# Attention and a gated feed-forward on one core: the product with T of six chunks in seven half products

## The chip, the core and the metric

The kernel runs on one core of a Trainium2 chip. The metric is the device time of one execution in microseconds. Before the change three runs gave a median of 410.5 us (409.81 to 410.56).

An instruction runs on one of five engines, each with its own queue that is served in order: TensorE (PE in the profile; its weight loads are PEld), VectorE (DVE), ScalarE (ACT), GpSimd (POOL) and SyncE (SP). SP, POOL and ACT also issue DMAs from their queues. TensorE writes to PSUM, which is read here by VectorE and ScalarE. GpSimd works on SBUF only.

## What is computed

Eight batches of eight heads, 1152 keys, and queries that are averaged in pairs (576 per batch and head), head size 64. The attention's result, 4608 tokens by 512, goes through a gated feed-forward:

```python
q_pool = q.reshape(B, H, S // 2, 2, D).mean(axis=3)
scores = scale * q_pool @ k.T
attn   = exp(scores - max) / sum
x      = attn @ v                 # as 4608 x 512
out    = (((x @ w1) * (x @ w2)) @ w3) @ w_out
```

w1 and w2 are 512 x 1024, w3 is 1024 x 1024, w_out 1024 x 512. The kernel multiplies T = w3 @ w_out once (1024 x 512), so that each token needs g = (x w1)(x w2), elementwise, and then g T.

## The kernel before, in words

**Attention.** Heads are taken in 32 pairs. The scores of all pairs form one long row of 32 x 9 x 576 columns, cut into 324 slots of 512. `scores` (L434) computes one slot for both heads of a pair into one of three double banks of PSUM (tag psc), and ScalarE writes the exponentials to a ring in SBUF (L448). An AV group (`av_mm`, L461) multiplies the ring with v: 18 matmuls of 65 columns (L474), or 36 for the rest tiles (L471). There are 144. VectorE normalizes each (L495 to L509), and a transpose turns the result into xT, on TensorE for the first pairs (L516, L519, copies L527 and L529), by a DMA on SP's queue from pair 8 on (`x_dma`, L485).

**Loads.** `prepare(p)` (L878) is written out at the start of pair p - 2. On GpSimd it casts K (L355), adds the query pairs (L359, L361) and casts V (L368). It issues the loads of V for pair p and of K and Q for p + 2, from GpSimd's queue for the first pairs, from SP's later. SP also turns K and Q by DMA (`transp`, L375).

**Feed-forward.** The 4608 tokens are nine chunks of 512 (CH). For chunks 0 to 6 (LATE is 7) `moe_groups(c)` (L597) yields steps: for each of eight blocks ft of 128 hidden columns, x w1 and x w2 (L583, 4 matmuls of 512 columns each), the first copied by VectorE (L610), the second multiplied with it into the gate tile g (L614); then four products g T for 128 tokens each (L621, 8 matmuls of 512 columns, called a step of size 2), scaled by VectorE (L630) and stored by GpSimd's queue (L595; for chunk 5 SP's, for chunk 6 SP's in pieces). T itself comes from `t_groups` (L544) ahead of chunk 0. Chunks 7 and 8 are done at the end by `late_chunks` (L683) in a form with seven half products for four (Strassen-Winograd): it needs sums of the four quarters of w1 and w2 (`weight_sums`, L649), of T (the tS tiles) and of x (`x_sums`, L670), all on GpSimd. The weight and T sums stand in one block at the start of pair 30.

**Order.** `_visits` (L184) is a planner that runs when the kernel is built. A visit is three score slots and then a string of A (an AV group), P (a pair's transposes on TensorE), m or s (a feed-forward step into the single bank mo, or into a bank of the scores). A beam search chooses the strings by the costs in `_Plan` (L115): time of TensorE, and when banks come free from VectorE and ScalarE. GpSimd and the DMA queues are not in it. The list `fills` (L920) gives each step's size; `free` says how many steps may be drawn after so many AV groups: a chunk's steps count as released when the tokens of the chunk are normalized and, with DMA transposes, four groups later. The steps themselves come from the generators in `queue`; `fill` (L831) takes the next, gives it a bank, issues its matmuls and then its VectorE work. What is left when the visits end is drawn between the last AV groups, and the rest behind them.

Tiles with a tag share buffers: a new one waits until all readers of the one `bufs` earlier are done (g8 holds the gates, two of them; kst, vst, qst the loads, two each).

Of the kernel before, what the change touches and what calls it, by code (L numbers as in the profile page):

```python
# [183 lines left out]
def _visits(n, start, units, pairs, fills, free, ready, width):  # L184
# [8 lines left out]
    for vis in range(n):  # L193
# [12 lines left out]
        def step(p, seq, na, f, pr, t0):  # L206
            d = p.t - t0
            loose = free[na] if vis >= start else 0
            if pr == len(ats) and (na >= len(units) or units[na][3] > vis) and (d > 1.0 or f >= loose):
                end(p, seq, na, f)  # L210
            if d > 2.3 or len(seq) > 4:
                return
            if pr < len(ats):
                q = p.copy()
                q.pair(ats[pr])
                step(q, seq + "P", na, f, pr + 1, t0)
            if na < len(units) and units[na][2] <= vis and seq.count("A") < 3:
                q = p.copy()
                q.av_group(*units[na][:2])
                step(q, seq + "A", na + 1, f, pr, t0)  # L220
            if f < loose:
                for b in "ms":
                    q = p.copy()
                    q.fill(fills[f][0], fills[f][1], b == "s")
                    step(q, seq + b, na, f + 1, pr, t0)
# [40 lines left out]
def kernel(  # L266
# [277 lines left out]
    def t_groups():  # L544
        w3T = {}

        def turn(ft):
            def go(pt):
                w3T[ft] = msb.tile([128, NF, 128], FP16, tag="w3T", bufs=2, name="w3T")
# [22 lines left out]
    CH = 512  # L572

# [22 lines left out]

    def moe_groups(c):  # L597
        t = {}

# [12 lines left out]
        for ft in range(NF):  # L612
            def gate(pb, ft=ft):
                nc.vector.tensor_tensor(out=t["g"][:, ft, :], in0=pb, in1=t["a"], op=ALU.mult)  # L614

            yield 1, lambda pa, ft=ft: first(pa, ft), keep, 0.0
            yield 1, lambda pb, ft=ft: proj(pb, w2sb, ft, c), gate, 0.0
# [23 lines left out]
    HF, HM, HC = NF // 2, dm // 2, CH // 2  # L641
    LATE = B * Sq // CH - 2
    IS = 1.0 / (SCL * SCL)
    wS, tS, xS = [], {}, {}
# [4 lines left out]
    def weight_sums():  # L649
        for w, tag in ((w1sb, "kst"), (w2sb, "vst")):  # L650
# [4 lines left out]
            nc.gpsimd.tensor_tensor(out=s1, in0=a21, in1=a22, op=ALU.add)  # L655
            minus(s2, s1, a11)
            minus(s3, a11, a21)
            minus(s4, a12, s2)
            wS.append({1: a11, 2: a12, 3: s4, 4: a22, 5: s1, 6: s2, 7: s3})
        b11, b12 = T16[:, 0:HF, 0:HM], T16[:, 0:HF, HM:dm]  # L660
        b21, b22 = T16[:, HF:NF, 0:HM], T16[:, HF:NF, HM:dm]
        st = [att.tile([128, 2, HF, HM], FP16, tag="qst", name="tS") for _ in range(2)]
        t1, t2, t3, t4 = st[0][:, 0], st[0][:, 1], st[1][:, 0], st[1][:, 1]
        minus(t1, b12, b11)
        minus(t2, b22, t1)
        minus(t3, b22, b12)
        minus(t4, b21, t2)
        tS.update({1: b11, 2: b21, 3: b22, 4: t4, 5: t1, 6: t2, 7: t3})

    def x_sums():  # L670
        st = msb.tile([128, 2, 4, NC // 2, HC], FP16, tag="wo", bufs=1, name="xS")
        for c in (0, 1):
            (_, a, n), = runs(LATE + c)
            b11, b12 = xT[:, 0:NC // 2, a:a + HC], xT[:, 0:NC // 2, a + HC:a + n]
            b21, b22 = xT[:, NC // 2:NC, a:a + HC], xT[:, NC // 2:NC, a + HC:a + n]
            x1, x2, x3, x4 = (st[:, c, i] for i in range(4))
# [154 lines left out]
    def fill(scored=False):  # L831
        if not head():
            return False
        n, go, put, at = ahead.pop(0)
        pt = bank(scored) if put else None
        go(pt)
        if put:
            put(pt)
        return True
# [19 lines left out]
    for _ in range(33):  # L859
# [61 lines left out]
    for ft in range(0, NF, 2):  # L921
        fills += [(0.5, W3_AT[ft // 2])] * 2 + [(1, WO_AT)] * 4
    free = []
    for n in range(NU + 1):
        for c in loose.get(n, []):
            fills += [(1, 0.0)] * (2 * NF) + [(2, 0.0)] * (CH // 128)
# [13 lines left out]
    def av_step():  # L940
# [9 lines left out]
        if p >= XD and t == QM - 1:  # L950
            x_dma(p)
        release()
# [102 lines left out]
```

## Time and profile before

| | us |
|---|---|
| median of 3 runs | 410.5 (409.81 to 410.56) |
| the profiled execution | 411.45 |
| its span, first to last instruction | 409.8 |
| TensorE busy | 396.8 (97%) |
| ScalarE busy | 335.2 (82%) |
| VectorE busy | 218.7 (53%) |
| GpSimd busy | 212.8 (52%) |
| matmuls of the product with T, L621 (192 in the main part, 32 in the last) | 45.6 and 7.2 |
| mean granted clock of TensorE | 0.998 |

Span and shares are of the profiled execution, which took 0.95 us more than the median of the runs; a difference worked out from the trace is taken from the median. Busy time of matmuls overlaps, since one begins before the one ahead has ended; so the distance from start to start is what a matmul takes of the engine's time. The profile's first part gives busy time by engine, its fourth the chain of work that ended last, its fifth groups of instructions by line: times executed, busy time, mean length of one, and the idle time of the engine just ahead of them with what ended it. The timeline lists merged instructions in order of time; the windows give busy time by stage.

### The profile page before, as it was taken

Reading aid. Unit: us, or ns where it says so; the run is one execution under the profiler, and the core shown is the slowest. Engines: PE = TensorE matmul, PEld = TensorE weight load, DVE = VectorE, ACT = ScalarE, POOL = GpSimd, SP = SyncE. Lnnn points to the kernel's source line nnn. Section 1 sums busy time; section 2 is a strip of 40 time slices with the busy share of each in tenths; the row PEclk is TensorE's granted clock in tenths of the full one; section 3 lists DMA queues with packets and bytes.
Section 4 is the critical chain, followed back from the end, with each engine's and each line's share of the span. In section 5 each row is a group of like instructions: output and inputs, shape, how many; then the busy total and the mean of one; then the engine's idle time right before and its main releaser. Section 6 shows DMA issues by size and latency. Waiting matters only on the chain.

```text
span 409.8 us, 13190 instructions
## 1 busy us (share of the span) xinstructions
PE 396.8 (97%) x5506; PEld 261.6 (64%) x5506; DVE 218.7 (53%) x594; ACT 335.2 (82%) x380; POOL 212.8 (52%) x237
## 2 busy tenths in 40 slices
PE   5899999999999999999999999999999999999995
PEld 3477887565555655565556556655777655658884
DVE  1255565665355534654355536553546435765993
ACT  4978979898889998999989999999899889107752
POOL 5789966470664225504533336333633897051860
PEclk9999999999999999999999999999999999999999
DMA  8999999999598899949999999996998170121005
GB/s 278 251 308 268 274 289 304 346 238 292 173 265 228 198 283 249 260 114 248 245 277 261 250 304 255 259 321 144 278 241 180 26 151 19 22 62 50 9 26 183
DMA packets 94079, 86.35 MB, mean 211 GB/s; under 512 B 60096, under 2 KB 68544, under 8 KB 94016
## 3 DMA queue, kind: packets, MB, share of 16 engines
q1 hardware_dynamic: 84480, 60.11, 61.3%
q0 software_dynamic: 8384, 24.06, 21.1%
q10 hardware_dynamic: 1152, 1.31, 0.9%
q8 instruction: 43, 0.70, 0.7%
q14 instruction: 20, 0.16, 0.1%
HBM read 67.11 MB, written 9.44 MB: 187 GB/s over the span
## 4 chain that ended last, share of the span: by engine, by line
PE 88%; DMA 6%; POOL 2%; ACT 1%; issue 1%; DVE 1%; SPq 0%; ACTq 0%
PE psc L443 19%; PE avb L474 16%; PE mo L583 15%; PE mo L621 10%; PE mot L583 9%; PE b L724 7%; PE mo L561 3%; DMA qst<-in_q_dram 3%; PE avb L471 3%; DMA xT<-xb 3%; PE b L621 2%; PE mo L724 1%; PE ptk L383 1%; ACT ring L448 1%; DMA kst<-in_k_dram 1%; PE avb L724 1%
## 5 line engine op out<-in xcount | busy, mean ns | idle before, releaser
L448 ACT ACTIVATE ring<-psc 128x1024 f16<-128x1024 f32 x324 | 308.2, 1025 | 34.5 <-PE psc L443 32.7
L474 PEld LDWEIGHTS <-ring 128*128 128x128 f16 x2304 | 84.4, 98 | 26.3 <-issue 7.1
L443 PE MATMUL psc<-kqT 64*128 64x512 f16 (+7 forms) x1152 | 96.2, 290 | 3.6 <-ACT ring L448 0.9
L474 PE MATMUL avb<-vaug,ring 128*128 128x65 f16 x2304 | 91.4, 193 | 0.0
L355 POOL CAST kq<-kst 128x1152 f16<-128x1152 f32 x31 | 35.7, 1152 | 77.1 <-DMA kqT<-kq 52.9
L443 PEld LDWEIGHTS <-kqT 64*128 64x128 f16 x1152 | 45.8, 95 | 31.2 <-issue 8.5
L621 PE MATMUL mo<-T,gT 128*128 128x512 f16 x192 | 45.6, 380 | 0.0
L495 DVE RECIPROCAL rzall<-avb 128x2 f32<-128x2 f32 x144 | 23.8, 165 | 37.0 <-PE avb L474 20.3
L630 DVE TENSOR_SCALAR osb<-mo 128x512 f32<-128x512 f32 x24 | 16.6, 692 | 48.6 <-PE mo L621 48.6
L359 POOL TENSOR_TENSOR kq<-qst 128x512 f16<-128x512 f32 x31 | 39.4, 1272 | 1.1 <-DMA qst<-in_q_dram 1.1
L368 POOL CAST vaug<-vst 128x1152 f16<-128x1152 f32 x32 | 36.6, 1143 | 5.8 <-PE psc L443 5.3
L595 POOL DMA_DIRECT2D out_dram<-osb x18 | 9.9, 552 | 55.9 <-DVE rzall L495 55.9
L614 DVE TENSOR_TENSOR gT<-mo,asb 128x512 f16<-128x512 f32 x36 | 24.9, 692 | 24.7 <-PE mo L583 24.4
L583 PE MATMUL mo<-xT,w2sb 128*128 128x512 f16 (+2 forms) x168 | 37.2, 350 | 0.0
L621 PEld LDWEIGHTS <-gT 128*128 128x128 f16 x224 | 19.8, 98 | 25.5 <-issue 5.2
L610 DVE COPY asb<-mo 128x512 f32<-128x512 f32 x32 | 22.1, 691 | 25.2 <-PE mo L583 24.9
L583 PEld LDWEIGHTS <-w2sb 128*128 128x128 f16 x256 | 21.9, 97 | 20.8 <-issue 4.2
L583 PEld LDWEIGHTS <-w1sb 128*128 128x128 f16 x256 | 22.0, 97 | 20.4 <-issue 3.9
L583 PE MATMUL mo<-xT,w1sb 128*128 128x512 f16 (+2 forms) x148 | 33.3, 351 | 1.1 <-DMA xT<-xb 1.1
L509 DVE TENSOR_TENSOR xb<-avb,rzall 128x128 f16<-128x128 f32 x96 | 28.0, 291 | 3.3
L583 PE MATMUL mot<-xT,w1sb 128*128 128x512 f16 (+1 forms) x104 | 23.6, 354 | 0.1
L583 PE MATMUL mot<-xT,w2sb 128*128 128x512 f16 (+1 forms) x84 | 19.5, 359 | 0.0
(143 smaller groups left out, 432.7 us busy)
## 6 DMA issues: line engine op xcount, KB each, us to landing
vst<-in_v_dram SPq DMA_DIRECT2D x25, 576.0 KB, 5.0
kst<-in_k_dram SPq DMA_DIRECT2D x23, 576.0 KB, 5.8
qst<-in_q_dram SPq DMA_DIRECT2D x23, 512.0 KB, 7.3
kst<-in_k_dram POOLq DMA_DIRECT2D x8, 576.0 KB, 9.9
out_dram<-osb POOLq DMA_DIRECT2D x18, 256.0 KB, 6.1
qst<-in_q_dram POOLq DMA_DIRECT2D x8, 512.0 KB, 10.6
vst<-in_v_dram POOLq DMA_DIRECT2D x7, 576.0 KB, 6.9
w3c<-in_moe_w_dram POOLq DMA_DIRECT2D x4, 512.0 KB, 8.2
```

Source lines behind the costliest of these rows:

```text
L355: nc.gpsimd.tensor_copy(out=kq16[:, 0:NJ].rearrange("p c u d -> p u c d"), in_=kst.rearrange("p u (c d) -> p u c d", d=D))
L359: eng.tensor_tensor(out=kq16[:, NJ:NJ + QM].rearrange("p c u d -> p u c d"), in0=qv[:, :, :, 0], in1=qv[:, :, :, 1], op=ALU.add)
L368: nc.gpsimd.tensor_copy(out=va[:, :, :, 0:D], in_=vs.pop(p).rearrange("p u (c d) -> p u c d", d=D))
L443: nc.tensor.matmul(psc[:, u, f - s * G:f - s * G + ln], kT2[u * 64:u * 64 + 64, jt, :], qpT[u * 64:u * 64 + 64, i0:i0 + ln], start=True, s ...
L448: nc.scalar.activation(out=ring[:, :, r0:r0 + G], in_=psc, func=AF.Exp, bias=0.0, scale=SCALE)
L474: nc.tensor.matmul(avb[:, o + u * E1:o + u * E1 + E1], ring[:, u, c0:c0 + 128], va[:, u, jt, :], start=(jt == 0 and u == 0), stop=(jt == N ...
L495: nc.vector.reciprocal(out=rzall[:, i, :], in_=av[:, :, D:E1].rearrange("p u o -> p (u o)"))
L509: nc.vector.tensor_tensor(out=xbt, in0=av[:, :, 0:D], in1=rzall[:, i, :].unsqueeze(2).to_broadcast([128, 2, D]), op=ALU.mult)
L583: nc.tensor.matmul(pw[:, d0:d0 + n], wt[:, mc, ft * 128:ft * 128 + 128], xT[:, mc, a:a + n], start=(mc == 0 and d0 == 0), stop=(mc == NC - ...
L614: nc.vector.tensor_tensor(out=t["g"][:, ft, :], in0=pb, in1=t["a"], op=ALU.mult)
L621: nc.tensor.matmul(po, t["g"][:, ft, tt:tt + 128], T16[:, ft, :], start=(ft == 0), stop=(ft == NF - 1))
L724: nc.tensor.matmul(pt[:, n * f:n * f + n], l[:, i, :], b[:, i, :], start=(p in (1, 5) and f == 0 and i == 0), stop=(i == kc - 1), skip_gro ...
```

## The change

The product with T of chunks 0 to 5 (`seven`) becomes seven products of 256 tokens by 256 columns over half the hidden columns: two blocks of 128 tokens, four matmuls of 256 columns each, in one bank. Product 1 is drawn behind gate 4, and products 2, 6, 7, 4, 5, 3 behind the first two steps of the next chunk (`LAG`). Sums of the gates are made on GpSimd, in place in g but for s1: behind gate 5 for two blocks, behind gates 6 and 7 for one, and a fourth sum behind product 2. Product 3 adds to the bank of product 5 after that has been read; both go to the bank mo ("m"). VectorE reads each product out with one operation, and each quarter of the chunk's output is stored from GpSimd's queue (`store_two`, one DMA for two blocks of 128 tokens where they lie together). The planner's list has 17 steps of size 1 for chunk 0, 23 for chunks 1 to 5, and 22 of size 1 with 4 of size 2 for chunk 6.

The T sums move to chunk 0's first four gates, the eight weight sums are issued one behind each AV group from pair 30 on. The T sums lie in the tile of w_out, the x sums in those of the Q loads. The matmuls that run ahead of the first transposes are 15 instead of 33.

```diff
@@ _visits
-                for b in "ms":
+                for b in fills[f][2]:
@@ moe_groups
+        lagged, late_fills[:] = late_fills[:], []
+        seven = c < LATE - 1
...
+        def product(pt, a, n, start=True):
+            for u in range(2):
+                for f in range(HF):
+                    nc.tensor.matmul(pt[:, u * HM:u * HM + HM], a[:, f, u * 128:u * 128 + 128], tS[n][:, f, :],
+                                     start=(start and u == 0 and f == 0), stop=(f == HF - 1), skip_group_check=True)
+
+        def plus(out, pt, x):
+            nc.vector.scalar_tensor_tensor(out=out, in0=two(pt), scalar=IS, in1=x, op0=ALU.mult, op1=ALU.add)
...
+        def quarter(h, n, pt, x):
+            osb = msb.tile([128, 2, HM], FP32, tag="osb", bufs=3, name="osb")
+            plus(osb, pt, x)
+            store_two(nc.gpsimd, c * CH + h * HC, osb, slice(n * HM, n * HM + HM))
...
+        def sums(f, n):
...
+            nc.gpsimd.tensor_tensor(out=s1, in0=a21, in1=a22, op=ALU.add)
+            minus(a21, a11, a21)
+            minus(a11, s1, a11)
+
+        def half(fts):
+            for ft in fts:
+                def gate(pb, ft=ft):
+                    nc.vector.tensor_tensor(out=t["g"][:, ft, :], in0=pb, in1=t["a"], op=ALU.mult)
+                    if c == 0 and ft < HF:
+                        t_sum(ft)
+                    if seven and ft > HF:
+                        sums(*((0, 2) if ft == HF + 1 else (ft - HF, 1)))
...
+                if 2 * ft + 2 == LAG:
+                    yield from lagged
+
+        yield from half(range(HF + 1))
+        if seven:
+            yield 1, lambda pt: product(pt, t["g"][:, 0:HF, 0:HC], 1), p1, 0.0
+        yield from half(range(HF + 1, NF))
...
+            def p2(pt):
+                quarter(0, 0, pt, t["p"])
+                for f in range(0, HF, 2):
+                    minus(g[:, HF + f:HF + f + 2, lo], g[:, HF + f:HF + f + 2, lo], g[:, f:f + 2, lo])
...
+            late_fills.extend((
+                (1, lambda pt: product(pt, g[:, HF:NF, lo], 2), p2, 0.0),
+                (1, lambda pt: product(pt, g[:, 0:HF, lo], 6), lambda pt: plus(t["p"], pt, t["p"]), 0.0),
+                (1, lambda pt: product(pt, g[:, 0:HF, hi], 7), p7, 0.0),
+                (1, lambda pt: product(pt, g[:, HF:NF, hi], 4), lambda pt: quarter(1, 0, pt, t["z"]), 0.0),
+                (1, p5, lambda pt: quarter(1, 1, pt, t["z"]), 0.0),
+                (1, lambda pt: product(t["bank"], g[:, HF:NF, lo], 3, False),
+                 lambda pt: quarter(0, 1, t["bank"], t["p"]), None),
+            ))
+            return
@@ weight_sums, one from av_step ahead of release()
+    def weight_sum():
+        if todo:
+            o, x, y, op = todo.pop(0)
+            nc.gpsimd.tensor_tensor(out=o, in0=x, in1=y, op=op)
@@ the matmuls ahead of the first transposes
-    for _ in range(33):
+    for _ in range(15):
@@ fills
-            fills += [(1, 0.0)] * (2 * NF) + [(2, 0.0)] * (CH // 128)
+            step = [(1, 0.0, "ms")]
+            rest = step * 4 + [(1, 0.0, "m")] * 2
+            fills += step * LAG + (rest if c else []) + step * (2 * NF - LAG)
+            fills += step if c < LATE - 1 else [(2, 0.0, "ms")] * (CH // 128)
```

## The prediction on record

> **What bounds the kernel now.** I read the shares first, then the chain that ended last, then the order of work in time on TensorE. In the page's first part:
>
> ```profile
> PE 396.8 (97%) x5506; PEld 261.6 (64%) x5506; DVE 218.7 (53%) x594; ACT 335.2 (82%) x380; POOL 212.8 (52%) x237
> ...
> PE 88%; DMA 6%; POOL 2%; ACT 1%; issue 1%; DVE 1%; SPq 0%; ACTq 0%
> ...
> L448 ACT ACTIVATE ring<-psc 128x1024 f16<-128x1024 f32 x324 | 308.2, 1025 | 34.5 <-PE psc L443 32.7
> ```
>
> PE is busy nearly throughout, the chain (second line) lies on PE for 88%, and ScalarE's exponentials wait 32.7 us for PE, not the other way round. A busy PE need not be a streaming PE, so I look at PE's timeline over one chunk's products with T:
>
> ```profile
> 99.39 1.90 PE L621 MATMUL mo<-T,gT 128*128 128x512 f16 x8
> 101.12 0.71 PE L474 MATMUL avb<-vaug,ring 128*128 128x65 f16 x18
> 101.67 0.22 PE L519 MATMUL avb<-both,xbc 128*128 128x64 f16 x2
> 101.83 0.83 PE L443 MATMUL psc<-kqT 64*128 64x384 f16 x10
> 102.58 1.90 PE L621 MATMUL mo<-T,gT 128*128 128x512 f16 x8
> 104.32 0.71 PE L474 MATMUL avb<-vaug,ring 128*128 128x65 f16 x18
> ```
>
> The columns are start and length; the ends are modelled, so the starts count. A visit (three score slots, one product, one AV group) repeats after 102.58 - 99.39 = 3.19 us and has no gap: 1.74 product, 0.55 AV, about 0.15 turn, 0.76 scores. A visit costs what PE does in it. Then the windows, cut at the starts of the chunks' first projections (66.14, 111.42, ...):
>
> ```profile
> 66.14:111.42 45.28, 45.14 (x620) 26.63 (x618) 25.44 (x76) 40.19 (x43) 23.48 (x27) 1.00 0.94 264
> 111.42:157.95 46.53, 46.42 (x678) 28.21 (x677) 23.56 (x69) 42.67 (x46) 18.22 (x21) 1.00 1.00 235
> 157.95:201.80 43.85, 43.76 (x611) 26.07 (x609) 22.12 (x61) 39.97 (x43) 19.68 (x22) 1.00 0.97 238
> ...
> 246.53:290.01 43.48, 43.48 (x614) 26.08 (x612) 22.05 (x61) 39.98 (x43) 19.44 (x23) 1.00 0.97 243
> ...
> 336.61:368.06 31.45, 31.45 (x379) 17.85 (x376) 20.08 (x55) 11.95 (x14) 14.73 (x11) 1.00 0.13 35
> ```
>
> After the window come its length and PE, PEld, DVE, ACT, POOL. PE has at most 0.14 us idle in each of these rows. From 290.01 to 336.61 it is the same; only at 205 us does PE stand, 1.06 us, for the transposed x of chunk 3. So a microsecond of PE work taken out is worth a microsecond, as long as ScalarE, banks and GpSimd keep up.
>
> **The change, step by step.** *Products.* Four products of 8 matmuls by 512 columns leave each of six chunks; seven of 8 by 256 come. From starts, the old one takes 1.74 us (102.58 to 104.32), four 6.95. The same shape as the new one runs at L561 (8 by 256; 61.59 to 62.47, 0.88) and L724 (four from 396.01 to 396.45, 0.109 each, 0.87 for 8):
>
> ```profile
> 61.59 1.04 PE L561 MATMUL mo<-wosb,w3T 128*128 128x256 f16 x8
> 62.47 0.71 PE L474 MATMUL avb<-vaug,ring 128*128 128x65 f16 x18
> ...
> 396.01 0.60 PE L724 MATMUL b<-tS,gT 128*128 128x256 f16 x4
> 396.45 0.60 PE L724 MATMUL b<-tS,room 128*128 128x256 f16 x4
> ```
>
> Seven are 6.16, so 0.79 goes per chunk, 4.7 us in six. There are 24 more weight loads per chunk; L724 has one for each matmul, and it shows at neither line.
>
> On this the Trainium skill speaks against the change: "TensorE: Matmul & The Clock Gate", Back-to-back issue gap, gives 131 ns for each matmul of 512 columns and 81 for 128 in a stream with weight loads. By it, 32 old matmuls would be 4.2 us and 56 new ones (about 98 ns between the two figures, an estimate) 5.5, a loss of 1.3 per chunk. The trace disagrees: 1.74 / 8 = 217 ns at 512 columns and 109 at 256.
>
> *Where the work goes.* Products 2 to 7 of a chunk are drawn two steps into the next. Counted in steps of 0.87, chunk 0's stretch goes from 24 to 17, those of 1 to 5 from 24 to 23, chunk 6's from 24 to 30. The windows of chunks 1 to 5 begin right behind the AV group that releases the chunk (groups 35, 57, 75, 93 and 111, counted in PE's timeline and held against the release counts in the code), so the planner already spends a chunk's steps by the next release, and shorter stretches are taken in full unless ScalarE is late next. ScalarE does six exponentials in 5.60 us (timeline from 10.87), 0.933 each, 2.80 per visit. Stretches of 13.5 visits need 37.8 and would have 42.6: covered. Chunk 0's has 14 visits, 39.2 on ScalarE, and 45.28 - 7 x 0.87 = 39.2 on PE: level. I take 0.5 us lost there, bounds 0 and 3.5 (below).
>
> *Evictions.* Seven instead of four, 0.69 each (L630, L614), 12.4 us on VectorE in all. A visit of two one-step fills (112.17 to 115.37, 3.20) takes as long as one with a two-step product, so more evictions and banks cost nothing there. Products 5 and 3 share a bank: product 3 waits for 5's eviction (0.2 + 0.69), hidden by an AV group and scores (0.55 + 0.76) if a visit lies between, about 0.3 lost in one visit. I take 0.
>
> *Sums on GpSimd.* The nearest rows, and the casts that share its queue:
>
> ```profile
> L814 POOL TENSOR_TENSOR room<-gT 128x512 f16<-128x512 f16 x6 | 6.8, 1158 | 10.5 <-PE b L724 9.2 <-DVE gT L783 1.3
> ...
> L647 POOL TENSOR_TENSOR tS<-T 128x1024 f16<-128x1024 f16 x2 | 4.3, 2135 | 0.0
> ...
> L368 POOL CAST vaug<-vst 128x1152 f16<-128x1152 f32 x32 | 36.6, 1143 | 5.8 <-PE psc L443 5.3 <-PE mo L583 0.4
> ...
> L355 POOL CAST kq<-kst 128x1152 f16<-128x1152 f32 x31 | 35.7, 1152 | 77.1 <-DMA kqT<-kq 52.9
> ```
>
> The first three are groups with shapes kept apart, the last is from the profile's page; the pair's other two sums take 1272 ns (L359) and 449 (L361). On the line through 512 and 1024 elements, 256 take 0.67 us. A chunk adds three sums behind gate 5 (3.5 us), three behind gate 6 (2.0), three behind gate 7 (2.0), two behind product 2 (2.3): 9.8, or 59 in six; stores of 256 pieces instead of 128 add perhaps 0.18 each (0.73 at L339 against 0.55 at L595), and chunk 5's four move here from SP's queue. POOL goes to about 67% of the span. What counts is the wait that comes new: product 6 needs the sums of gate 7. From that gate's last matmul to product 6 PE does AV 0.56, scores 0.76, two steps 1.75, AV 0.65, scores 0.76, product 2 0.88: 5.4, less 0.9 for the eviction, 4.5 us. The sums take 2.0, so 2.5 are free. In front of them can stand one pair's casts, 1.15 + 1.27 + 0.45 + 1.14 = 4.0: then product 6 is 1.5 late, and PE with it, and all queued behind it, scores included. Behind waiting sums on POOL stand the next casts; SP holds that pair's loads until them, and the transposes of x for the next chunk stand behind these in SP's queue. But those casts ran up to a pair (some 11 us) ahead, so there is room. I take 0.5 in all, bounds 0 and 9.0 (below).
>
> *Weight sums.* Eight of 2.13 us move from one block (319.8 to 336.7) to one behind each AV group from pair 30; four T sums go to chunk 0's gates, where POOL is half idle. They are needed at 368, so the span does not see them; what they do to chunk 5's sums is in the rival. The x sums change only buffers (those of the last q loads, cast at 312).
>
> *Start.* 18 warm-up matmuls go. PE waits 1.27 us for GpSimd's cast at 4.71 anyway, so 0. Matmuls run at half rate until about 18.7 us with 33 (14 transposes 1.65 us at 14.70, 0.95 at 25.53), so the warm-ups do not set the clock; bounds -1 and +1 for a different moment.
>
> **Sum**: -4.7 + 0.5 + 0.5 = -3.7 us. The profiled execution took 411.45 (span 409.8), so 407.75; against the median of 410.5 that is **406.8**.
>
> **Rivals.** *GpSimd late (slower).* A pair starts every 3.375 visits (5184 columns of scores, 512 to a slot); pairs 9, 18, 22 and 26 start in the last two visits of chunks 0, 2, 3 and 4, so the 4.0 us of casts can stand between gate 6's and gate 7's sums: 1.5 us each. At the end of chunk 5 sums of 7.5 and three weight sums (6.4) share 10.9 us between gate 5 and product 6: 3.0 late. All five: 9.0. It decides from 4.7. Three casts and chunk 5: 7.5, so 410.5 - 4.7 + 7.5 = **413.3**. For it: POOL is in order and the planner has no term for it. Against: the casts depend on nothing late, and fit where the gates are spread. 0.26.
>
> *ScalarE takes it back.* If chunk 0's stretch loses its second fill visit by visit, each becomes 0.76 + 0.56 + 0.88 + 0.1 = 2.3 on PE and 2.8 on ScalarE: 0.5 lost in seven visits, 3.5; with 0.5 for GpSimd 410.5 - 4.7 + 4.0 = **409.8**. Against: visits of two AV groups and one fill (130.52 to 133.39, 2.87) fit ScalarE. 0.08; 0.04 more for between this and the forecast.
>
> *Weight loads show.* If 24 loads of 98 ns per chunk (PEld, L724) stood in the open: 2.35 x 6 = 14.1, so 410.5 - 4.7 + 14.1 = **419.9**. L724 speaks against; 0.02. The 131 and 98 ns of the Trainium skill (that same section) would end at 410.5 + 6 x 1.3 = 418.3; this trace's 217 and 109 are against it, and it lies within the 0.02.
>
> **How the numbers follow.** Forecast 0.60, all of it faster. 0.2% of 410.5 is 0.8 us, about what a measurement of this kernel can tell from no change. Faster 0.60 + 0.04 = 0.64, same 0.08, slower 0.26 + 0.02 = 0.28. Low end: 410.5 - 4.7 with the 1.06 us at 205 us gone too, 404.7; high end the first rival's 413.3, with half of its chance above. The forecast's own range is 404.7 to 408.7.
>
> **What would show it.** Right: half products of 0.88 us; each stretch of chunks 1 to 5 0.8 shorter, chunk 0's about 6 and the last about 5 longer; no PE wait on POOL above 1 us. Wrong: a product waiting for POOL's sums at each boundary; ScalarE without gaps and PE waiting for it between 60 and 110 us; PE waiting for the transposes of x by more than 1 us.

## The result, and the profile after

The changed kernel takes 409.83 us (median of 13 runs, 408.96 to 410.82), the kernel before beside it 410.72 (13 runs, 409.81 to 411.16): a ratio of 0.9977, 95% interval 0.9967 to 0.9986. It is faster by 0.9 us, or 0.2%, where 3.7 us were forecast; the time lies outside the forecast's own range (404.7 to 408.7) and inside that of the rivals. Two more sets of runs of the same kernel, each beside the kernel before on another chip, gave 0.9976 (0.9966 to 0.9986) and 0.9974 (0.9962 to 0.9985); their expectations:

> The changed kernel unaltered, on the chip and beside the runs of this call, for the comparisons within it and for a second profile: 0.9960 to 0.9995 of before. Theory A in its GpSimd part expects that the wait of chunk 5's product 6 for POOL differs from execution to execution (0.69 us in the first profile, the mean of all runs being about 1.3 us longer than that profile's gain): in this profile between 0.3 and 3 us.

> The changed kernel unaltered, as the measure for the other three on this chip: 0.997 to 0.998 of the kernel before.

The profiles of these two sets have the waits of the first one at the same places: the longest, of product 6 of chunk 5 (below), is 0.69 us in the first profile, 0.69 and 0.71 in these.

The profiled execution after took 409.23 us (span 407.6), the one before 411.45 (409.8). The traced pair differs by 2.2 us, the medians by 0.9: the traced run of before took longer than each of the 13 that its median is made of, and it alone of the two has a wait of 1.06 us for the transposed x. Below, sizes come from medians where they can and from the traces for the place.

From the profile's page after, the shares, the chain that ended last, and the group of the exponentials:

```profile
PE 392.2 (96%) x5632; PEld 275.5 (68%) x5632; DVE 230.8 (57%) x610; ACT 336.6 (83%) x384; POOL 282.0 (69%) x319
...
PE 89%; ACT 4%; POOL 3%; DVE 2%; issue 1%; DMA 1%; ACTq 0%; POOLq 0%
...
L448 ACT ACTIVATE ring<-psc 128x1024 f16<-128x1024 f32 x324 | 307.8, 1027 | 29.0 <-PE psc L443 27.4
```

PE's busy time fell by 4.6 us, the span by half of that. On the chain ScalarE rose from 1% to 4%, and the idle time of the exponentials fell from 34.5 to 29.0 us: the room on ScalarE has been used up, in part. GpSimd went from 52% to 69%.

The products take what was forecast. PE's timeline at the head of chunk 1, with two half products of chunk 0 (start and length first):

```profile
111.23 1.05 PE L633 MATMUL mo<-T,gT 128*128 128x256 f16 x8
112.11 1.04 PE L633 MATMUL mot<-tS,gT 128*128 128x256 f16 x8
112.99 0.71 PE L474 MATMUL avb<-vaug,ring 128*128 128x65 f16 x18
```

From start to start that is 0.88 each. Adding up such distances over the whole timeline, the products of chunks 0 to 5 take 37.3 us against 41.8 before: 4.5 less, where 4.7 were forecast. The windows run from the start of visit 20 to visit 32, to visit 47, and from visit 89 to visit 104 (visits counted from 0):

```profile
70.18:107.26 37.08, 36.19 (x540) 22.05 (x539) 22.34 (x70) 33.77 (x37) 30.38 (x29) 1.00 0.98 266
107.26:153.38 46.12, 46.04 (x719) 31.01 (x718) 26.12 (x74) 42.64 (x46) 28.96 (x33) 1.00 0.96 240
...
283.51:330.49 46.98, 46.95 (x760) 36.28 (x756) 26.75 (x72) 42.97 (x46) 31.55 (x33) 1.00 0.70 159
```

The columns are those of before's windows: length, PE, PEld, DVE, ACT, POOL. The steps of T, ahead of chunk 0, are spread over two more visits, so its stretch begins at 70.18 (visit 20) instead of 66.14 (visit 18). Both kernels end it at visit 32, at 107.26 instead of 111.42: 4.2 us are gained by then, where 6 were forecast. In its 12 visits PE is idle for 0.89 us in all, where before had 0.14 in 14. ScalarE is busy there for 33.77 of 37.08 us. The later stretches do not each get 0.8 shorter: the one from 283.51 is 46.98 where before had 46.60, because in the planner's new order it holds more projections (x w1 and x w2) than before, 16.2 us against 14.2. From visit 107 on the changed kernel takes 3.3 us longer than before, with the steps left over, as was forecast in kind.

The waits stand in PE's timeline. In chunk 0's stretch:

```profile
98.80 0.39 PE L443 MATMUL psc<-kqT 64*128 64x512 f16 x2 [0.27 <-ACT ring L448]
...
101.55 0.39 PE L443 MATMUL psc<-kqT 64*128 64x128 f16 x4 [0.24 <-ACT ring L448]
```

The scores wait there for a bank that ScalarE has still to read: 0.8 us in three waits, and 1.1 with one in chunk 2's stretch; before had none at these places. The timeline marks only waits above 0.15 us. Shorter ones lie between the starts of the matmuls themselves: all scores from visit 3 on take 85.6 us from start to start against 84.5 before. One wait for GpSimd is new, at product 6 of chunk 5. It stands first in PE's timeline; the second fence is GpSimd's queue ahead of it:

```profile
333.35 0.72 PE L633 MATMUL mot<-tS,gT 128*128 128x256 f16 x5 [0.69 <-POOL gT L732]
```

```profile
329.05 2.13 POOL L747 TENSOR_TENSOR wS<-w1sb 128x1024 f16<-128x1024 f16 x1
331.13 0.67 POOL L657 TENSOR_TENSOR s<-gT 128x256 f16<-128x256 f16 x1
...
332.63 0.67 POOL L732 TENSOR_TENSOR gT<-s,gT 128x256 f16<-128x256 f16 x1
```

A weight sum stands right ahead of the sums of gate 7. Where the traced 2.2 us are, in sums of the distances from start to start (after less before):

| | us |
|---|---|
| products of chunks 0 to 5 | -4.5 |
| wait for the transposed x, gone | -1.06 |
| scores from visit 3 on, hidden waits included | +1.1 |
| shown waits for ScalarE, chunks 0 and 2 | +1.10 |
| wait of product 6 of chunk 5 | +0.69 |
| first 20 visits: a later start (0.40), longer waits (0.62) | +1.0 |
| AV, transposes, projections and the rest | -0.6 |

### The profile page after: what moved, and what is told of

Read it like the earlier page. It is cut to its first block, busy times and chain, and to the rows that moved or that the text cites. A ratio compares the mean times of both kernels' runs of the same rounds, so it can differ in the third digit from the quotient of the medians.

```text
span 407.6 us, 13533 instructions
## 1 busy us (share of the span) xinstructions
PE 392.2 (96%) x5632; PEld 275.5 (68%) x5632; DVE 230.8 (57%) x610; ACT 336.6 (83%) x384; POOL 282.0 (69%) x319
## 3 DMA queue, kind: packets, MB, share of 16 engines
q10 hardware_dynamic: 1152, 1.31, 1.0%
## 4 chain that ended last, share of the span: by engine, by line
PE 89%; ACT 4%; POOL 3%; DVE 2%; issue 1%; DMA 1%; ACTq 0%; POOLq 0%
PE psc L443 20%; PE avb L474 17%; PE mo L587 12%; PE mot L587 9%; PE b L811 7%; PE mo L633 6%; ACT ring L448 3%; PE mo L561 3%; PE mot L633 3%; PE avb L471 2%; PE b L587 2%; PE b L709 2%; PE ptk L383 2%; POOL wS L747 2%; PE mo L811 1%
## 5 line engine op out<-in xcount | busy, mean ns | idle before, releaser
L443 PE MATMUL psc<-kqT 64*128 64x512 f16 (+7 forms) x1152 | 97.6, 291 | 5.1 <-ACT ring L448 2.2
L443 PEld LDWEIGHTS <-kqT 64*128 64x128 f16 x1152 | 46.8, 95 | 34.3 <-issue 12.7
L657 POOL TENSOR_TENSOR s<-gT 128x256 f16<-128x256 f16 (+1 forms) x18 | 14.9, 828 | 37.5 <-DVE gT L664 27.9
L633 PEld LDWEIGHTS <-gT 128*128 128x128 f16 x288 | 26.3, 98 | 8.5 <-issue 3.9
L732 POOL TENSOR_TENSOR gT<-gT 128x512 f16<-128x512 f16 (+1 forms) x30 | 28.6, 963 | 1.5
L587 PE MATMUL mot<-xT,w1sb 128*128 128x512 f16 (+1 forms) x124 | 27.8, 352 | 0.0
L628 DVE COPY asb<-mo 128x512 f32<-128x512 f32 x25 | 17.3, 692 | 16.6 <-PE mo L587 16.3
L587 PE MATMUL mo<-xT,w1sb 128*128 128x512 f16 (+1 forms) x116 | 25.9, 351 | 0.0
L628 DVE COPY asb<-mot 128x512 f32<-128x512 f32 x27 | 18.7, 692 | 5.0 <-PE mot L587 5.0
L901 POOL TENSOR_TENSOR room<-gT 128x512 f16<-128x512 f16 x6 | 6.8, 1155 | 18.7 <-PE b L811 17.4
```

Source lines behind the costliest of these rows:

```text
L443: nc.tensor.matmul(psc[:, u, f - s * G:f - s * G + ln], kT2[u * 64:u * 64 + 64, jt, :], qpT[u * 64:u * 64 + 64, i0:i0 + ln], start=True, s ...
L587: nc.tensor.matmul(pw[:, d0:d0 + n], wt[:, mc, ft * 128:ft * 128 + 128], xT[:, mc, a:a + n], start=(mc == 0 and d0 == 0), stop=(mc == NC - ...
L628: nc.vector.tensor_copy(out=t["a"], in_=pa)
L633: nc.tensor.matmul(pt[:, u * HM:u * HM + HM], a[:, f, u * 128:u * 128 + 128], tS[n][:, f, :], start=(start and u == 0 and f == 0), stop=(f ...
L732: nc.gpsimd.tensor_tensor(out=out, in0=x, in1=y, op=ALU.subtract)
```

## The experiments

**Theory A**: the 4.5 us are really taken from PE, and ScalarE takes some 2 of them back, because the put-off products leave the early stretches too short for it; GpSimd's sums take another part. **Rival B**: ScalarE takes little, and the loss lies elsewhere (the sums' load on GpSimd, the order, the start). The expectations give theories A and B anew for each run. Kernels that leave a part of the computation out are run for their time alone, since their output is not the right one.

**ScalarE out of the way.** From slot 27 on, the exponentials of one head of each pair only, in the changed kernel and in the kernel before:

```diff
-        nc.scalar.activation(out=ring[:, :, r0:r0 + G], in_=psc, func=AF.Exp, ...)
+        nc.scalar.activation(out=ring[:, 0, r0:r0 + G], in_=psc[:, 0], func=AF.Exp, ...)   # slots 27 and on
```

> The changed kernel with its order of work untouched, but from slot 27 on ScalarE takes the exponential of one head of each pair only (512 of 1024 columns; the other half of the ring keeps older values), so ScalarE is out of the way. To be read against the same edit in the kernel before. Theory A (ScalarE's pace takes the gain back: with six products of each chunk drawn a chunk later, the stretch of chunk 0 has 17 steps instead of 24, and the score slots of the shorter visits wait for ScalarE): without ScalarE the change is worth nearly what the products save, this kernel 3.3 to 4.8 us under the same edit of before, and no PE wait on the exponentials is left. Theory B (GpSimd's sums, VectorE's seven read-outs or the start take it back): the difference stays at 0.5 to 2 us, as it is with the full exponentials.

> The kernel before with the same cut of ScalarE's work (one head of each pair from slot 27 on). Its product visits of 3.19 us already cover ScalarE's 2.80, so both theories expect little here: 0 to 2 us under the kernel before (408.7 to 410.7). It is the base line for the first run: theory A expects the changed kernel with the same cut 3.3 to 4.8 us under this, theory B 0.5 to 2.

Measured: 405.07 us, 0.9856 (0.9841 to 0.9870), and 407.93, 0.9924 (0.9911 to 0.9937). With ScalarE out of the way the change is worth 2.9 us, with it 0.9: ScalarE takes back 2.0, by the intervals of the ratios with an uncertainty of about 0.9. The 2.9 lie between the two theories' numbers (3.3 to 4.8, 0.5 to 2): ScalarE is the largest loss, but not all of it. In the traces no wait for ScalarE is left from visit 20 on in either of them, and the scores from visit 3 on take 82.3 and 82.4 us.

The kernel before gains more than the 0 to 2 us expected of it: 2.8 us by medians. Its scores shrink from 84.5 to 82.4 us, all in single visits (the median visit is unchanged). One of them in PE's timelines, first before, then with half the exponentials:

```profile
123.92 1.09 PE L443 MATMUL psc<-kqT 64*128 64x512 f16 x10
```

```profile
124.11 0.83 PE L443 MATMUL psc<-kqT 64*128 64x512 f16 x10
```

So some 2.1 us of waiting for ScalarE lay in the kernel before already, in pieces too short for the timeline to mark, and counted there as busy PE. The 97% of PE on the page was not all work. Half the exponentials also halve what ScalarE reads and writes; that the scores shrink in single visits, and not everywhere, speaks for waits.

**GpSimd without the sums.** The products take the gates as they are:

```diff
-                    if seven and ft > HF:
-                        sums(*((0, 2) if ft == HF + 1 else (ft - HF, 1)))
...
-                for f in range(0, HF, 2):
-                    minus(g[:, HF + f:HF + f + 2, lo], g[:, HF + f:HF + f + 2, lo], g[:, f:f + 2, lo])
...
-                product(pt, t["s1"], 5)
+                product(pt, g[:, 0:HF, hi], 5)
```

> The changed kernel without the sums of the gates on GpSimd (the eleven operations per chunk are left out and the products take the gates as they are; order, matmuls, read-outs and stores stay). Theory A (ScalarE): only the one wait of 0.7 us on POOL goes, the time is 0 to 1.0 us under the changed kernel's, 0.9953 to 0.9980 of before. Theory B in the form that GpSimd gives the gain back: 2 us or more under the changed kernel, below 0.993 of before.

> The kernel without the gates' sums on GpSimd once more, beside the changed kernel on the same chip. If the 1.6 us are real: 1.2 to 2.0 us under the changed kernel in the same call. If only the visible wait of 0.7 us counts: 0.4 to 1.0 us under it.

Measured: 408.67 us, 0.9937 (0.9925 to 0.9950), and, beside the changed kernel on one chip, 408.90 us against 410.14, 0.9957 (0.9942 to 0.9973) against 0.9974. By the ratios that is 1.6 us the first time and 0.7 the second. So the sums cost about 1.2 us, with an uncertainty of 0.8. In the trace all that differs from the changed kernel between visits 20 and 107 is the wait of product 6, 0.69, and 0.18 in the half products that follow it; the visits from 20 to 103 agree within 0.1 us in sum. What lies between these 0.9 us and the 1.2 stays open.

**Neither ScalarE nor sums**: half the exponentials (as above) and no sums.

> The changed kernel without the sums of the gates on GpSimd and with the exponentials of one head only from slot 27 on (both parts of the computation are left out, so the time alone counts). Theory A: the 0.9 us of the change are 4.5 us from the products, less about 2.0 us that ScalarE takes back and about 1.6 us for GpSimd's sums; then with both covers gone the gain over the kernel before with half exponentials (ratio 0.9924) is the whole 4.5 us: ratio 0.981 to 0.983, about 403.2 us. Theory B: the 1.6 us between the run without sums and the changed kernel are no cost of the sums on the path but one 0.7 us wait and the moment; then this run stands 0.7 us under the one with half exponentials alone (0.9856): ratio 0.983 to 0.985, about 404.4 us.

Measured: 404.37 us, 0.9865 (0.9815 to 0.9915); one of the four runs took 408.88 and widens the interval. Both expectations are within it or at its edge, so this run decides nothing.

**What the sums cost, by result or by load.** The sums are made, but into a tile that no product reads:

```diff
-            minus(a21, a11, a21)
-            minus(a11, s1, a11)
+            minus(s1, a11, a21)
+            minus(s1, a22, a11)
```

with product 5 reading g, and the fourth sum going to s1 too.

> The changed kernel with the sums of the gates still made on GpSimd, in the same number and size, but written to a tile that no product reads; the products take the gates as they are (the computation is changed there, so the time alone counts). GpSimd's queue is as busy as in the changed kernel, and no product waits for it. Theory A (products wait for the sums' results): as the kernel without sums, ratio 0.9935 to 0.995. Theory B (the load itself costs: casts come later, or the sums disturb other engines' access to SBUF): as the changed kernel, 0.997 to 0.998. Theory C (there is no cost but the one wait of 0.7 us, and the rest was the moment): 0.7 us under the changed kernel, wherever that and the kernel without sums stand on this chip.

Measured: 410.52 us, 0.9995 (0.9984 to 1.0006), not faster than the changed kernel and outside all three expectations. Product 6's wait is gone, and 0.9 us with it, but 1.4 us come back behind visit 107: the product with T of chunk 6 now waits for gates (0.9 us in three waits). These stand on VectorE behind three operations of the kernel's final test, which use SBUF only. Two of them in VectorE's timelines, first in this kernel, then in the one without sums:

```profile
356.06 1.25 DVE L1095 TENSOR_SCALAR ok<-rzall 128x288 f32<-128x288 f32 x1
357.35 1.34 DVE L1096 TENSOR_TENSOR ok<-ok 128x288 f32<-128x288 f32 x1
```

```profile
354.25 0.30 DVE L1091 TENSOR_SCALAR ok<-rzall 128x288 f32<-128x288 f32 x1
354.58 0.46 DVE L1092 TENSOR_TENSOR ok<-ok 128x288 f32<-128x288 f32 x1
```

Here they take 1.25 and 1.34 us, while GpSimd makes the x sums without a pause (351.35 to 360.8). In the kernel without sums GpSimd has a gap just then (353.56 to 355.70, it waits for x), and they take 0.30 and 0.46. So this run does not separate a sum's result from its load: what it saves at product 6 it loses in the tail.

**Weight sums later**, behind the last gate's sums:

```diff
-        if todo:
+        if todo and (len(todo) > 7 or avn[0] > 132):
```

> The changed kernel with seven of the eight weight sums begun four AV groups later, behind the sums of chunk 5's last gate instead of ahead of them. TensorE's order is the same. If the wait of product 6 of chunk 5 (0.7 us in the trace) is the only cost of the weight sums: 0.7 us under the changed kernel, ratio 0.9955 to 0.9965. If the trace shows only a part of what GpSimd's queue costs in other executions: up to 1.6 us, 0.9935. If it is covered elsewhere: no difference, 0.9975.

> The changed kernel with seven of the eight weight sums begun four AV groups later, once more, as the measure for the other run: 0.995 to 0.9965 of the kernel before, where the changed kernel stood at 0.9974 to 0.9977 in four calls.

Measured: 409.02 us, 0.9956 (0.9942 to 0.9970), the changed kernel beside it at 410.14; and 409.63, 0.9970 (0.9958 to 0.9982). Product 6's wait is gone in both traces, and 0.6 of its 0.9 us come back at chunk 6's product with T, as above. These are the lowest times of a complete kernel here, but their intervals overlap with the changed kernel's: a gain of some tenths is likely, and not shown.

**The gates of chunk 6 ahead of the test** on VectorE, added to the late weight sums:

```diff
+    for _ in range(5):
+        fill()
     ok = const.tile([128, 2, NQ], FP32)
```

> The changed kernel with seven weight sums begun four AV groups later, and the last five gate steps of chunk 6 drawn ahead of VectorE's operations on rzall and ok (the test of the sums at the end), which stood in front of them on VectorE. Theory A (in the tail VectorE's operations in SBUF stand while GpSimd makes the x sums, and hold chunk 6's gates): product 1 of chunk 6 no longer waits for a gate, 0.4 to 0.7 us under the run with late weight sums alone: ratio about 0.994 to 0.995. Theory B (the gates come late for another reason): as that run, 0.9955; the wait of TensorE for gT stays.

Measured: 410.02 us, 0.9981 (0.9971 to 0.9991). The wait for chunk 6's gates is gone, as A has it, but the test comes later and PE now waits for its outcome; from the list of PE's waits:

```profile
PE avb L811 <- DVE badi L1109: 0.7, 1, 0.7
```

So it is right that the gates were late because they stood behind the test, and the cure is none: the delayed operations only meet another reader.

**Weight sums in one block** at pair 30:

```diff
                     weight_sums()
+                    while todo:
+                        weight_sum()
...
-        weight_sum()
```

> The changed kernel with the eight weight sums in one block at the start of pair 30, as in the kernel before, instead of one behind each AV group. The block is 8 x 2.13 = 17 us on GpSimd from about 324 us on, and the sums of gate 7 of chunk 5 would stand behind it, until about 343 us; product 6 stands at 333 us. Theory A (GpSimd's queue is the limit at chunk 5): PE waits about 9 us there, some of it given back later, and matmuls run slower for a while behind it: 8 to 14 us over the changed kernel, ratio 1.017 to 1.032. Theory B (there is slack and order on GpSimd does not matter): as the changed kernel, 0.9977.

Measured in two runs: 423.52 us, 1.0294 (1.0245 to 1.0343), as A has it. Product 6 waits 11.2 us, and PE's granted clock is 0.50 behind it (window 344 to 348):

```profile
344.44 1.25 PE L633 MATMUL mot<-tS,gT 128*128 128x256 f16 x5 [11.17 <-POOL gT L732]
```

GpSimd's order does decide at chunk 5, as the forecast's rival had it; spreading the weight sums leaves 0.7 of these 11.

**The order**: products 2 to 7 in their own chunk's stretch.

```diff
-            late_fills.extend((
+            yield from ((
...
-            fills += step * LAG + (rest if c else []) + step * (2 * NF - LAG)
-            fills += step if c < LATE - 1 else [(2, 0.0, "ms")] * (CH // 128)
+            fills += step * 2 * NF
+            fills += step + rest if c < LATE - 1 else [(2, 0.0, "ms")] * (CH // 128)
```

> The changed kernel with products 2 to 7 drawn in their own chunk's stretch, right behind the last gate, so that stretches have 23 steps each (chunk 6: 24) and none of it is put off. Theory A expects that the ScalarE waits go (some 2.3 us), but product 6 now follows the last gate by one product and the scores, 2.2 us less 0.9 for the read-out, while the sums of that gate take 2.0 on GpSimd, with up to 4.0 of casts ahead: 0.7 to 2 us of waits for POOL at each of six chunks, 4 to 12 in all; time 407 us plus that less 0.7, so 409 to 416. What the putting off buys is then the difference in POOL waits. Theory B without ScalarE: slower than the changed kernel by the POOL waits alone, 4 us or more, with ScalarE waits unchanged.

Measured: 429.13 us, 1.0442 (1.0412 to 1.0472), longer than the 409 to 416 of A; B had named 4 us or more. Casts of a pair stand ahead of gate 7's sums, and product 6 waits up to 3.4 us. Over all six chunks the waits for GpSimd come to 11.1 us in the trace, and the clock falls behind four of them. PE's timeline behind one such wait, and the windows there (PEclk is the third column from the right):

```profile
242.68 0.72 PE L633 MATMUL mot<-tS,gT 128*128 128x256 f16 x5 [3.37 <-POOL gT L732]
243.23 1.10 PE L474 MATMUL avb<-vaug,ring 128*128 128x65 f16 x18
244.27 1.46 PE L443 MATMUL psc<-kqT 64*128 64x512 f16 x10
```

```profile
240.00:244.00 4.00, 1.32 (x21) 1.27 (x22) 0.57 (x1) 0.48 (x1) 3.84 (x7) 0.92 0.78 288
244.00:248.00 4.00, 4.00 (x36) 2.56 (x34) 1.28 (x4) 2.85 (x3) 2.44 (x3) 0.66 0.15 35
```

After the wait the granted clock is 0.66, and the scores take 1.46 us instead of 0.83. From starts, the AV group, the scores and the product behind the wait take 0.49, 0.63 and 0.52 longer than elsewhere: the wait costs its length and 1.6 us more. On this the Trainium skill ("TensorE: Matmul & The Clock Gate", Why this matters for your kernels) says that idle gaps of more than about 3 us take TensorE's clock down; the trace agrees at 3.37 us. But in the same run the clock fell to 0.85 and 0.72 (windows 104 to 108 and 108 to 112) behind a wait of 1.83 us with one of 0.59 just ahead of it.

The same with no sums at all, so that nothing waits for GpSimd:

> The changed kernel with products 2 to 7 in their own chunk's stretch, and without the sums of the gates on GpSimd (the products take the gates as they are; the computation is changed there, so the time alone counts). Nothing waits for GpSimd here, so the order alone shows. Theory A: the 2.0 us that ScalarE takes back come mostly from putting the products off (chunk 0's stretch is left with 17 steps for its 14 visits, and 6 steps end where ScalarE has nothing to do); then this run is 1.3 to 2.3 us under the run without sums in the late order (ratio 0.9937): ratio 0.988 to 0.9905, 406.2 to 407.2 us. Theory B: ScalarE's share is spread over all stretches and does not hang on the order: 0.993 to 0.9945, 408.2 to 408.8 us.

Measured: 411.37 us, 1.0008 (0.9987 to 1.0029), and so neither theory's number: above the late order without sums, by 2.1 to 2.9 us (0.9957 and 0.9937). Much of ScalarE's share does go: the scores from visit 3 on take 84.4 us, 1.2 less than in the changed kernel and as in the kernel before, and the shown waits for ScalarE shrink by 0.4. Against that stand two new waits for gates, 0.9 in sum, and the tail: it has nothing to draw any more behind the last AV group, and PE stands there until VectorE has done the final test:

```profile
365.96 0.16 PE L1101 MATMUL avb<-ones,okh 128*1 128x1 f16 x1 [2.27 <-DVE ones L1098]
```

```profile
364.00:368.00 4.00, 2.04 (x13) 1.59 (x14) 1.94 (x8) 1.14 (x2) 0.00 (x0) 0.83 0.20 51
368.00:372.00 4.00, 4.00 (x30) 3.17 (x28) 0.34 (x1) 2.21 (x5) 0.00 (x0) 0.74 0.24 59
```

2.27 us of waiting, and 1.7 us more for the late chunks at a granted clock of 0.83 and 0.74. The put-off steps are thus not only a loss of ScalarE's time: they are what hides the test in the tail.

**Four steps instead of two** (`LAG = 4`):

> The changed kernel with products 2 to 7 drawn four steps instead of two into the next chunk's stretch: product 6 comes about one visit (3 us) later, so GpSimd's sums have that much more room. Theory A (GpSimd's sums cost about 1.6 us, of which the wait of 0.7 us of product 6 of chunk 5 is the visible part): that wait goes, and 0.7 to 1.6 us with it: 408.2 to 409.1 us, ratio 0.9935 to 0.996. Theory B (the sums cost nothing beyond what the trace of the changed kernel shows, and the rest is the moment): at most 0.7 us: 409.1 to 409.8 us, ratio 0.996 to 0.9977.

Measured: 412.54 us, 1.0035 (1.0014 to 1.0055), neither theory's number. Product 6's wait is gone, but in the order that the planner now finds, the first projection of chunk 3 starts at 196.96, 3.0 us earlier than in the changed kernel (199.96), and its last matmul has to wait for x:

```profile
198.95 0.38 PE L587 MATMUL mo<-xT,w1sb 128*128 128x512 f16 x1 [1.18 <-DMA xT<-xb]
```

At the end 1.6 us of waits for chunk 6's gates come on top. The traced run of before had the same wait for x, at the same step; in the changed kernel the step stands behind the DMA. So a slack that the planner does not know decides over a microsecond.

**The sums of gates 6 and 7 on VectorE**, in their own stretch and put off:

```diff
         def sums(f, n):
+            eng = nc.gpsimd if n == 2 else nc.vector
...
-            nc.gpsimd.tensor_tensor(out=s1, in0=a21, in1=a22, op=ALU.add)
+            eng.tensor_tensor(out=s1, in0=a21, in1=a22, op=ALU.add)
```

and the two differences behind it in the same way.

> Products 2 to 7 in their own chunk's stretch again (23 steps each, nothing put off), but the three sums behind gates 6 and 7 run on VectorE, right behind the gate on the same engine, instead of behind casts in GpSimd's queue; the sums of gate 5 and the fourth sum stay on GpSimd. Theory A (the gain went to ScalarE's pace, because the putting off empties chunk 0's stretch, and to waits for GpSimd's queue): both are gone, so the products' 4.5 us show less 0.5 to 1.5 us: 406.5 to 408 where before takes 411, 0.9895 to 0.9930 of before, faster than both kernels. If the run without putting off was slow for another reason than GpSimd's queue (banks, VectorE's read-outs, the transposes of x), this one is slow as well, above 1.01.

> The changed kernel, products put off as there, with the sums behind gates 6 and 7 on VectorE. Takes away the wait of product 6 for GpSimd's queue and a third of GpSimd's added work, and leaves ScalarE's part. Theory A: like the run without gate sums, 1 to 2 us under the changed kernel, 0.9930 to 0.9955 of before, and 1.5 to 3 us slower than the run with own stretches and VectorE's sums. If it equals that run, the putting off costs nothing.

Measured: 431.72 us, 1.0512 (1.0487 to 1.0537), and 442.96, 1.0776 (1.0752 to 1.0800), against expectations that both missed. Timeline of the second, all engines:

```profile
105.39 5.32 DVE L659 TENSOR_TENSOR gT<-gT 128x256 f16<-128x256 f16 x1
...
105.62 1.14 POOL L368 CAST vaug<-vst 128x1152 f16<-128x1152 f32 x1
...
109.43 1.14 POOL L368 CAST vaug<-vst 128x1152 f16<-128x1152 f32 x1
...
111.69 1.87 PE L587 MATMUL mo<-xT,w2sb 128*128 128x512 f16 x4 [5.35 <-DVE asb L628]
...
114.65 0.29 DVE L659 TENSOR_TENSOR gT<-gT 128x256 f16<-128x256 f16 x1
...
157.38 1.24 DVE L659 TENSOR_TENSOR gT<-gT 128x256 f16<-128x256 f16 x1
```

One operation takes 0.29 us where GpSimd is idle, and 5.32 where GpSimd runs a pair's three casts and two sums without a pause (105.62 to 110.57). Everything behind it on VectorE, and so PE, stands. The 5.32 is the only case of its kind in the two runs. At the next chunk's boundary the three operations take 1.08, 1.24 and 1.51 us, each ending about when GpSimd's operation beside it ends, and PE waits 3.79 us. At the other four it waits 2.2 to 5.1.

**The start**: 33 warm-up matmuls instead of 15.

```diff
-    for _ in range(15):
+    for _ in range(33):
```

> The changed kernel with 33 matmuls ahead of the first transposes, as before. The first transposes wait for GpSimd's cast of the first K (4.7 to 5.1 us) in both, and the moment at which matmuls turn fast differs between profiles without regard to the count. Expected by all theories: the changed kernel's time, 0.9960 to 0.9995 of before; below 0.9955 the shorter warm-up would have cost something.

Measured: 410.31 us, 0.9991 (0.9979 to 1.0004). More of them bring no gain; whether they cost some tenths is within the interval.

## Why the forecast was right in sign and wrong in size

*Products, -4.7*: measured -4.5 (0.88 each). Right. The weight loads do not show, and the rival that they would is out.

*ScalarE, "I take 0.5 us lost there, bounds 0 and 3.5"*: measured 2.0, the difference of 2.9 us (half exponentials) and 0.9. **This is the step that failed**: 1.5 of the 2.8 us that are missing. The mechanism was the one named, and the place too: about 1.3 us of it lie in chunk 0's stretch. The size was taken from a balance in sum (39.2 us on ScalarE, 39.2 on PE), as if equal sums meant no loss. In sum there was even room, since the planner left 12 visits with 33.77 us of ScalarE in 37.08. But the work comes in visits: where PE has less than ScalarE's 2.80 us or little more, it waits, and a fuller visit later does not give that back. The second half of the step, that "shorter stretches are taken in full unless ScalarE is late next", held for chunks 1 to 5 only in part: hidden waits of some 0.7 us and a shown one of 0.3 lie there. The reading under it, that a visit "costs what PE does in it" and that ScalarE waits for PE and not the other way round, was not quite true of the kernel before either: 2.1 us of its scores were waits for ScalarE. The rival "ScalarE takes it back" had the mechanism, with 3.5 us and a chance of 0.08; the truth lies between it and the forecast. That its 409.8 is the time measured is in part luck: it has ScalarE too dear by 1.5 us, the sums too cheap by 0.4 to 0.7 and the start at nothing.

*GpSimd, "I take 0.5 in all, bounds 0 and 9.0"*: one wait of 0.69, 0.87 with what follows it, about 1.2 by medians. The rival saw where: chunk 5, behind the weight sums, but priced it at 3.0, and 1.5 for each of four pairs whose casts could stand ahead; at these four no wait is in the trace. What it rests on is real: with the weight sums in one block the wait is 11.2 us. That removing the wait (late weight sums) gives back 0.6 of it in the tail, where VectorE is held beside the x sums, is nowhere in the forecast.

*Start, 0 (-1 to +1)*: in the traced pair visit 3 starts 0.4 us later, and the waits from there to visit 20 are 0.6 longer: together 1.0, at the edge of the bounds. The 0.4 is no property of the change, since visit 3 starts at 16.28 in the trace of before and at 16.83 in that of before with half the exponentials, which differs only behind it. The 0.6 comes from the order: the planner now has scores right behind the transposes of K at 25.4, where before has a step of T between, and they wait 0.78 us for K's turned tiles. All traces of this order have that wait. The number of warm-ups is not the cause.

*Evictions, weight loads, the shared bank of products 5 and 3*: 0, as forecast; no wait for them is in the list.

*From the trace to the median.* The sum was made against 411.45 and carried over by a constant 0.95. But the traced run held 1.06 us of waiting for x, which the trace of the same kernel with half exponentials does not have; it is in the 2.2 us of the traced pair, and little of it can be in the 0.9 of the medians. How often the kernel before has that wait is open, since other executions of it were not traced.

In sum: -4.5 + 2.0 + 0.9 to 1.2 + 0.6 for the start gives -1.0 to -0.7, and the medians have -0.9. This is less of a test than it looks, because the 2.0 is itself the 2.9 less the 0.9 of the medians, and the costs of ScalarE and of the sums are each uncertain by some 0.8.

## What to carry to other kernels

Work taken from one engine is worth its time only visit by visit, up to what the next engine needs in that same visit; sums that are equal over a stretch already mean a loss, and here even 3 us of room in sum did not prevent one. Waits too short for a trace to mark count as busy; halving the other engine's work, in both kernels, brings them out. Steps put off are not neutral: they take cover from the stretch they leave, and give cover to the one they reach, so look at both ends (here ScalarE's stretch, and the final test in the tail). Sums on a side engine need a place in its queue as well as time, and VectorE is no substitute for GpSimd where both work in SBUF at once.

## What the runs showed of the hardware

A VectorE operation with two inputs in SBUF (128 x 256, f16) took 0.29 us beside an idle GpSimd and 5.32 us beside three casts and two sums of GpSimd in a row; f32 operations of 288 columns went from 0.30 and 0.46 to 1.25 and 1.34 us beside GpSimd's x sums. VectorE's reads from PSUM with one input in SBUF kept their 0.69 us beside GpSimd's work (104.05, L665, in the run with the sums put off on VectorE). The Trainium skill ("SBUF — State Buffer", SBUF: two separate sides) says that VectorE, with two inputs in SBUF, and GpSimd share one pair of ports there, locked by whichever starts first for its whole instruction, while the other blocks. The traces agree that it blocks. As a rule VectorE gets in when one GpSimd operation has ended, or a short one and the one behind it: 1.08, 1.24 and 1.51 us at the second boundary, beside GpSimd operations of 0.49 to 1.31. Once, with 5.32, it did not get in between one operation and the next and stood until GpSimd's row of five had ended. Why that one did is open.

TensorE's granted clock fell after a wait of 1.83 us with one of 0.59 ahead of it (windows of 0.85 and 0.72) and after one of 2.27 us (0.83 and 0.74), as after 3.37 us (0.92 and 0.66). But length alone does not decide: in the run with products in their own stretch, the same test makes PE wait 2.27 us at 385.12, and the windows from 384 to 392 are at 1.00. What a fall cost beyond the wait itself was nearly the same each time: 1.7 us after 2.27, 1.6 after 3.37, and, from starts, 2.0 after 11.17. The clock lost in the two windows of 4 us is as large, for example (0.17 + 0.26) x 4 = 1.7.
